# Second half's first two query/key/value column groups by seven products, and two weight buffers allocated ahead of a third

## The chip, the cores and the metric

The kernel runs on one core of one Trainium2 chip. The metric is the device time of one execution in microseconds, from three runs. The engines are TensorE (PE; its weight loads are listed as PEld), VectorE (DVE), ScalarE (ACT), GpSimd (POOL) and SyncE (SP), which here issues the DMAs.

## What is computed

A transformer block whose attention and MLP run side by side on the same layer norm; 2048 tokens, width 576, 32 heads of 18, 8 keys per query at a dilation of 2, hidden width 4608.

```python
xn = _layernorm(x)
q, k, v = (xn @ wqkv) split into 32 heads of 18
idx = pos[:, None] - 2 * arange(8)[None, :]
o = softmax(q . k[idx] * 18 ** -0.5) . v[idx]
attention = o.reshape(S, 576) @ wo
h = xn @ w1 + b1
mlp = (h * tanh(softplus(h))) @ w2
out = x + attention + mlp
```

## The kernel before

**Precision.** Every float32 matrix is held as a high and a low part. A product of two 128-deep tiles is three matmuls (high by high, low by high, high by low). The depth of 576 is four tiles of 128 and a remainder of 64, whose high and low rows share one tile, so that it costs two matmuls. A full product of 128 tokens with 432 columns is thus 4 x 3 + 2 = 14 matmuls.

**Stages.** The 2048 tokens are two halves (`hf` 0 and 1), a half is two blocks `b` of 512, a block is four token tiles `jj` of 128. In each half the program normalises and transposes the tokens (`norm1`, `ln_transpose`, tags `ta` and `tb`), makes q, k and v, and runs the MLP in 18 quads of 256 hidden columns: `m1_part` makes the hidden products (tags `h`), activates them, and `p_item` multiplies by w2 (tags `po`). The last `p_item` chunks of half 0 stand at the start of half 1's q/k/v work. The output projection of the attention comes last.

**q, k, v.** The 1728 columns are four groups `g` of 432. `qkv_item` makes one group of one token tile directly (14 matmuls, tags `pq`); ACT copies the result out of the accumulator. In both halves groups 0 and 1 go this way, and groups 2 and 3 go by Strassen's scheme with seven products in Winograd's form: the two blocks of 512 tokens, the two groups and the two halves of the depth make a 2 x 2 problem. One token tile of it takes seven products of six or eight matmuls, 50 in all, where four direct products take 56. It needs sums of the tokens (`S`, made by `s_step` on POOL, `s_high` on ACT, `s_low` on DVE) and sums of the weights (tags `y`, made at the start of half 0). Half 0 runs it with `za_part`, product by product over all token tiles: B11, B21, T2, T3, T4, T1, B22. Half 1 runs it with `z_part`, token tile by token tile, with weights that half 0 wrote to DRAM (`z_fetch`). A result that starts a q/k/v tile is copied by ACT, one that is added to it is added by DVE; `qkv_send` then stores it to DRAM.

**Attention.** A generator, stepped at listed places of the plan (`STEPS`, `SUMS`). For eight pairs of units per half POOL multiplies q by k (`pr`) and weights by v (`pv`), DVE reduces (`L`, `og`) and does the softmax's sums, ACT the exponentials. The last pairs of half 0 run beside half 1's q/k/v work.

**What sets the order.** The program is a list `plan` of PE's work in slots. `before(slot, fn)` hangs loads, casts, sums and steps on slots, and the tables `MOVED`, `STEPS`, `SUMS` and `AHEAD` shift single ones. Every engine executes what it was given in the written order. All DMAs go through one SP queue in order, and each waits also for one of eight semaphores in turn, so no more than eight are under way. Line numbers below are those of the kernel before.

**Buffers.** The weights of a quad's hidden products lie in `wa` (two buffers `wa0`, `wa1` of 5120 bytes per partition, written as separate tags), `t` (width 4 tiles) and `wc`. A tag's place is fixed when its first buffer is allocated. The tag `r3`, a 3456-byte weight buffer of the seven products, is allocated first; in the built program it starts at byte 206400 of each partition, `wa0` at 209856 and `wa1` at 217280. Counted from a multiple of 256, `wa0` and `wa1` start 192 bytes on; `r3`, `t`, `wc`, the token tiles `xt` and the sums `S` start 64 bytes on.

Of the kernel before, what the change touches and what calls it, by code (L numbers as in the profile page):

```python
# [18 lines left out]
P = 128  # L19
NH = 2  # L20
SH = S // NH
NB = 2
# [19 lines left out]
 108: (0, 0),  # L42
 117: (1, 1),
 122: (1, 1),
 131: (0, 1, 0),
 138: (0, 0),
 143: (0, 0),
 144: (0, 0),
 217: (0, 0),
 238: (-2, 1),  # L50
 282: (0, 0),
 389: (0, 0),
 424: (0, 0),
 430: (-1, 1),
 489: (0, 0),
 535: (0, 0),
 617: (1, 1),
 619: (1, 1),
 632: (0, 0),
 649: (1, 1),  # L60
 650: (-2, 1),
 692: (-1, 1),
 749: (0, 0),
 757: (0, 0),
 761: (0, 0),
 766: (-2, 0),
 789: (0, 0),
 810: (1, 1),
 815: (-1, 1),
 849: (0, 0),  # L70
 856: (0, 0),
 860: (-1, 1),
 887: (0, 0),
 889: (0, 0),
 945: (0, 0),
 957: (0, 0),
 961: (0, 0),
 997: (0, 0),
 1001: (2, 1),
 1011: (0, 1, 0),  # L80
 1012: (0, 0),
 1023: (0, 0),
 1025: (-2, 0),
 1041: (2, 1),
 1050: (1, 1),
 1071: (0, 0),
 1162: (0, 0),
 1184: (1, 1),
 1191: (0, 0),
 1208: (0, 0),  # L90
 1218: (2, 1),
 1221: (-2, 1),
 1229: (0, 1, 0),
 1253: (1, 1),
 1307: (0, 0),
 1328: (0, 0, 0)}


STEPS = ((36, 41, 47, 49, 53, 57, 63, 67, 70, 77, 78, 83, 85, 91, 95, 98, 105, 107, 111, 117, 123, 127, 130, 137, 139, 143,
# [7 lines left out]
SUMS = {(0, 0): (38, 0),  # L107
# [3 lines left out]
 (0, 33): (174, 0),  # L111
 (0, 59): (237, 0),
 (1, 5): (267, 0),
 (1, 8): (276, 0),
 (1, 10): (279, 0),
 (1, 28): (324, 0),
 (1, 35): (340, 0),
 (1, 38): (346, 0),
 (1, 46): (371, 1),
 (1, 50): (382, 1),  # L120
 (1, 54): (392, 0),
 (1, 56): (397, 1)}
AHEAD = (35, 37, 39, 40, 80, 84, 173, 184, 233, 234, 239, 240, 242, 244, 301, 318, 320, 339, 340, 416, 417)
# [7 lines left out]
def block_kernel(ctx: ExitStack, tc: tile.TileContext, x, wq, wo, w1, b1, w2, mask, out):  # L131
# [154 lines left out]
    def ln_transpose(hf, b, jj):  # L286
# [6 lines left out]
        if b == 0:  # L293
            nc.gpsimd.tensor_copy(rem, xn[:, KT * P:])
        else:
            nc.gpsimd.tensor_tensor(out=rem, in0=rem, in1=xn[:, KT * P:], op=ALU.subtract)
# [27 lines left out]

    def new(kind, hf, i):
        tag, bufs, width = home(kind, i)
        if tag == "wc":
# [110 lines left out]
    def qkv_item(hf, g, b, jj, mid=None, mid_at=4):  # L438
# [7 lines left out]
        if (g, b, jj) == (NQ - 1, 0, JB - 1):  # L446
            pq = ps.tile([P, 512], F32, tag="out", bufs=4, name=f"pq_{n}_{jj}")
        else:
            pq = ps.tile([P, 512], F32, tag="h", bufs=4, name=f"pq_{n}_{jj}")
# [13 lines left out]
        if jj == JB - 1:  # L463
            if (hf, g, b) == (1, 1, 1):
                zq["send"] = lambda: qkv_send(hf, g, b, kvs, qs)
            else:
                qkv_send(hf, g, b, kvs, qs)
# [66 lines left out]
    def za_part(n, half):  # L534
        X0, X1 = XTs[0, 0], XTs[0, 1]
        name = YORDER[n]
        src, hi, lo, rest = {"B11": (X0, 0, 5, None), "B21": (X0, 2, 7, (X0, 4, "R2")), "T2": (Ss.get((0, 1)), 0, 2, None),
                             "T3": (X1, 0, 5, None), "T4": (X1, 2, 7, (X1, 4, "R2")),
                             "T1": (Ss.get((0, 0)), 0, 2, (X1, 4, "R3")),
                             "B22": (Ss.get((0, 2)), 0, 2, (X1, 9, "R3"))}[name]  # L540
        to, add_ = {"B11": ((2, 0), 0), "B21": ((2, 0), 1), "T2": ((2, 1), 0), "T3": ((3, 1), 0), "T4": ((2, 1), 1),
                    "T1": ((3, 1), 1), "B22": ((3, 0), 0)}[name]
        if half == 0 and not add_:
            yq[to] = (sb.tile([P, 2 * UQ, JB, CU], F32, tag="w2", bufs=4, name="ykv_%d_%d" % to),
                      sb.tile([P, (TJ + HALO) * CU], F32, tag="kv", bufs=4, name="yqs_%d_%d" % to)[
                          :, 0:UQ * JB * CU].rearrange("p (u j c) -> p u j c", u=UQ, j=JB))
        kvs, qs = yq[to]
        for jj in (2 * half, 2 * half + 1):
            tok = slice(jj * P, (jj + 1) * P)
            if name == "B11":  # L550
                yq["h1", jj] = ps.tile([P, 512], F32, tag="out", bufs=4, name=f"y1_{jj}")[:, 0:432]
            elif name in ("B21", "T3"):
                yq["h3", jj] = ps.tile([P, 512], F32, tag="h", bufs=4, name=f"y{name}_{jj}")[:, 0:432]
            h = yq["h3" if name in ("B21", "T3", "T4") else "h1", jj]
            seq = [(src[:, xs + k, tok], yw[name, k][:, wl]) for k in range(2) for xs, wl in ((hi, 0), (lo, 0), (hi, 1))]
            if rest is not None:
                seq += [(rest[0][:, rest[1], tok], yw[rest[2], 0][:, wl]) for wl in range(2)]
# [9 lines left out]
        if half and (add_ or name == "B22"):  # L567
            qkv_send(0, *to, kvs, qs)
# [15 lines left out]

    def z_part(hf, jj, part):
        X0, X1 = XTs[hf, 0], XTs[hf, 1]
        tok = slice(jj * P, (jj + 1) * P)
        if part == 0:
            if jj == 0:
                for g in (2, 3):  # L590
                    for b in range(NB):
                        zq[g, b] = (sb.tile([P, 2 * UQ, JB, CU], F32, tag="w2", bufs=4, name=f"zkv_{g}_{b}"),
                                    sb.tile([P, UQ, JB, CU], F32, tag="xn", bufs=XNB, name=f"zqs_{g}_{b}"))
            if jj == JB - 1:
                zq["h"] = [ps.tile([P, 512], F32, tag="out", bufs=4, name=f"z{n}_{jj}")[:, 0:432] for n in (1, 3)]
                zq["h"].append(ps.tile([P, 512], F32, tag="h", bufs=4, name=f"z2_{jj}")[:, 0:432])
            else:
                zq["h"] = [ps.tile([P, 512], F32, tag="h", bufs=4, name=f"z{n}_{jj}")[:, 0:432] for n in (1, 3, 2)]
        h1, h3, h2 = zq["h"]
        S1, S2, S4 = (Ss[hf, n] for n in range(3))  # L600

        def mul(h, X, hi, lo, name, first, rest=None):
            seq = [(X[:, xs + k, tok], zw[name, k][wl]) for k in range(2) for xs, wl in ((hi, 0), (lo, 0), (hi, 1))]
            if rest is not None:
                seq += [(rest[0][:, rest[1], tok], zw[rest[2], 0][wl]) for wl in range(2)]
            for n, (l, r_) in enumerate(seq):
                nc.tensor.matmul(h, l, r_, start=first and n == 0, stop=n == len(seq) - 1, skip_group_check=True)  # L607

        def views(g, b, h):
            kvs, qs = zq[g, b]  # L610
            return ((kvs[:, :, jj, :], h[:, 0:288].rearrange("p (u c) -> p u c", u=2 * UQ)),
                    (qs[:, :, jj, :], h[:, 288:432].rearrange("p (u c) -> p u c", u=UQ)))

        def snap(g, b, h):
            for d, v in views(g, b, h):
                nc.scalar.copy(d, v)

        def plus(g, b, h):
            for d, v in views(g, b, h):
                nc.vector.tensor_tensor(out=d, in0=v, in1=d, op=ALU.add)  # L620

        def send(g, b):
            if jj == JB - 1:
                qkv_send(hf, g, b, *zq[g, b])
        if part == 0:
            mul(h1, X0, 0, 5, "B11", True)
            snap(2, 0, h1)
            mul(h2, X0, 2, 7, "B21", True, (X0, 4, "R2"))
            plus(2, 0, h2)
            send(2, 0)  # L630
        elif part == 1:
            mul(h1, S2, 0, 2, "T2", False)
            snap(2, 1, h1)
            mul(h3, X1, 0, 5, "T3", True)
            snap(3, 1, h3)
        elif part == 2:
            mul(h1, S1, 0, 2, "T1", False, (X1, 4, "R3"))
# [1151 lines left out]
```

## Time and profile before

| what | value |
|---|---|
| three runs | 1113.59, 1114.18, 1112.23 us (median 1113.59) |
| the profiled execution's own time | 1110.76 us |
| its span, first to last instruction | 1109.0 us |
| granted TensorE clock | 0.998 |
| busy: PE, PEld | 1094.4 us (99%), 1005.4 us (91%) |
| busy: DVE, POOL, ACT | 874.6 us (79%), 780.1 us (70%), 508.7 us (46%) |
| DMA | 276.01 MB, mean 249 GB/s |

Profile and prediction use times from the span's start. In a group's row, `out<-in` are the tiles written and read; "idle" is the time for which the engine stood still just before, with what it then waited for. A window's row gives each engine's busy time in that stretch and the number of its instructions, then the granted clock, the DMA engines' busy share and their rate.

### The profile page before, as it was taken

Reading aid. Unit: us, or ns where it says so; the run is one execution under the profiler, and the core shown is the slowest. Engines: PE = TensorE matmul, PEld = TensorE weight load, DVE = VectorE, ACT = ScalarE, POOL = GpSimd, SP = SyncE. Lnnn points to the kernel's source line nnn. Section 1 sums busy time; section 2 is a strip of 40 time slices with the busy share of each in tenths; the row PEclk is TensorE's granted clock in tenths of the full one; section 3 lists DMA queues with packets and bytes.
Section 4 is the critical chain, followed back from the end, with each engine's and each line's share of the span. In section 5 each row is a group of like instructions: output and inputs, shape, how many; then the busy total and the mean of one; then the engine's idle time right before and its main releaser. Section 6 shows DMA issues by size and latency. Waiting matters only on the chain.

```text
span 1109.0 us, 18148 instructions
## 1 busy us (share of the span) xinstructions
PE 1094.4 (99%) x6478; PEld 1005.4 (91%) x6478; DVE 874.6 (79%) x1433; ACT 508.7 (46%) x935; POOL 780.1 (70%) x635
## 2 busy tenths in 40 slices
PE   8999999999999999999999999999999999989998
PEld 8998899999999999999998889989999989989998
DVE  6775888898987888987756568887888895787786
ACT  5554554454456444454333354444444434243353
POOL 2434967878776776867679669778676799967442
PEclk9999999999999999999999999999999999999999
DMA  6769997867877586666598899675668476487864
GB/s 225 271 232 344 358 327 247 273 241 265 273 250 249 209 280 220 232 251 203 186 303 276 272 339 337 239 237 200 212 216 266 167 241 219 152 292 243 252 218 141
DMA packets 183006, 276.01 MB, mean 249 GB/s; under 512 B 53346, under 2 KB 124292, under 8 KB 182916
## 3 DMA queue, kind: packets, MB, share of 16 engines
q1 hardware_dynamic: 182916, 274.86, 73.4%
q8 instruction: 51, 0.84, 0.3%
q14 instruction: 39, 0.32, 0.1%
HBM read 162.16 MB, written 112.66 MB: 248 GB/s over the span
## 4 chain that ended last, share of the span: by engine, by line
PE 92%; DMA 2%; DVE 2%; issue 1%; POOL 1%; SPq 1%; ACT 0%; DVEq 0%; ACTq 0%; POOLq 0%
PE h L834 29%; PE po L936 21%; PE po L1028 12%; PE pq L459 7%; PE po L1049 6%; PE h L840 6%; PE o L1232 5%; PE z L607 4%; PE y L559 1%; PE yT L559 1%; PE yB L559 1%; DMA pw<-kept_T 1%; DMA kept_yB<-yw_B 1%; DMA w<-kept_w 1%; PE ta L166 0%
## 5 line engine op out<-in xcount | busy, mean ns | idle before, releaser
L936 PEld LDWEIGHTS po<-w,act 128*128 128x128 f32 x1728 | 236.5, 188 | 5.7
L936 PE MATMUL po<-w,act 128*128 128x288 f32 x1728 | 240.6, 295 | 0.0
L697 POOL TENSOR_TENSOR pr<-q,kv 128x576 f32<-128x576 f32 x128 | 195.6, 1553 | 10.2 <-DMA q<-q_d 4.6
L736 POOL TENSOR_TENSOR pv<-L,kv 128x576 f32<-128x576 f32 x128 | 176.5, 1477 | 31.6 <-DVE L L729 14.5
L886 POOL TENSOR_TENSOR act<-c,act 128x512 fp32r<-128x512 f32 x69 | 93.7, 1358 | 99.6 <-ACT act L885 94.1
L1028 PEld LDWEIGHTS po<-pw,u 128*128 128x128 f32 x1008 | 138.3, 188 | 5.5 <-issue 1.9
L1028 PE MATMUL po<-pw,u 128*128 128x288 f32 x1008 | 140.7, 295 | 1.5 <-DMA pw<-kept_T 1.5
L940 DVE TENSOR_TENSOR acc<-po,acc 128x288 f32<-128x288 f32 x288 | 118.5, 449 | 23.1 <-PE po L936 21.8
L834 PE MATMUL h<-xt,t 128*128 128x512 f32 x432 | 111.3, 392 | 2.1 <-ACT t L365 1.5
L834 PE MATMUL h<-S,t 128*128 128x512 f32 x432 | 110.4, 391 | 0.1
L834 PE MATMUL h<-xt,wa 128*128 128x512 f32 x432 | 106.2, 395 | 0.0
L880 ACT ACTIVATE c<-c,b1c 128x512 f32<-128x512 f32 x69 | 50.0, 725 | 121.5 <-DVE c L879 121.3
L742 DVE TENSOR_REDUCE og<-pv 128x144 f32<-128x1152 f32 x64 | 86.0, 1345 | 19.4 <-POOL pv L736 19.3
L702 DVE TENSOR_REDUCE L<-pr 128x64 f32<-128x1152 f32 x64 | 85.9, 1342 | 17.6 <-POOL pr L697 17.5
L834 PEld LDWEIGHTS h<-xt,wa 128*128 128x128 f32 x432 | 81.3, 189 | 18.5
L834 PEld LDWEIGHTS h<-xt,t 128*128 128x128 f32 x432 | 79.0, 188 | 18.1 <-ACT t L365 1.9
L459 PE MATMUL pq<-wq,xt 128*128 128x432 f32 x448 | 91.8, 362 | 0.8 <-ACT xt L172 0.7
L834 PEld LDWEIGHTS h<-S,t 128*128 128x128 f32 x432 | 78.0, 188 | 13.4 <-ACT rm L868 0.5
L459 PEld LDWEIGHTS pq<-wq,xt 128*128 128x128 f32 x448 | 83.0, 188 | 5.6 <-ACT xt L172 1.1
L1049 PEld LDWEIGHTS po<-w,act 128*128 128x128 f32 x576 | 79.9, 191 | 5.0 <-DVE accP L1052 3.4
L1049 PE MATMUL po<-w,act 128*128 128x288 f32 x576 | 81.2, 298 | 2.9 <-DVE accP L1052 2.9
L868 ACT COPY c<-h 128x512 f32<-128x512 f32 x69 | 40.4, 585 | 86.5 <-PE h L840 43.5
(259 smaller groups left out, 1989.2 us busy)
## 6 DMA issues: line engine op xcount, KB each, us to landing
kv<-kv_d SPq DMA_DIRECT2D x64, 396.0 KB, 6.1
kept_t<-t SPq DMA_DIRECT2D x36, 512.0 KB, 4.1
t<-kept_t SPq DMA_DIRECT2D x36, 512.0 KB, 4.6
pw<-kept_T SPq DMA_DIRECT2D x24, 576.0 KB, 6.1
rw<-in_w SPq DMA_DIRECT2D x36, 320.0 KB, 5.0
kept_wa<-wa SPq DMA_DIRECT2D x18, 640.0 KB, 4.6
wa<-kept_wa SPq DMA_DIRECT2D x18, 640.0 KB, 5.2
rw<-in_w SPq DMA_DIRECT2D x36, 288.0 KB, 5.7
```

The source lines that it names most:

```text
L459: nc.tensor.matmul(pq[:, 0:432], XT[:, xi, tok], wt[wi][:, hl, 0:432], start=i == 0, stop=i == len(seq) - 1)
L697: nc.gpsimd.tensor_tensor(out=pr[:, x:x + hh], in0=q[:, j0 + x:j0 + x + hh, None, :].to_broadcast([P, hh, W, CU]), in1=win(kt, 0, CU, j0 + ...
L702: nc.vector.tensor_reduce(L[:, k, j0:j0 + hj].rearrange("p j w h -> p (j w h)"), pr.rearrange("p j w (h d) -> p (j w h) d", h=2), axis=AX, ...
L736: nc.gpsimd.tensor_tensor(out=pr[:, x:x + hj].rearrange("p j d w -> p j w d"), in0=L[:, k, x:x + hj, :, h:h + 1].to_broadcast([P, hj, W, DH]),
L742: nc.vector.tensor_reduce(og[:, c0:c0 + DH, :].rearrange("p d j -> p j d"), pr, axis=AX, op=ALU.add)
L834: nc.tensor.matmul(ph, wt[:, wl, wk * P:(wk + 1) * P], X[:, xs, :], start=first and i == 0, stop=last and i == len(seq) - 1, skip_group_ch ...
L840: nc.tensor.matmul(ph, wt[:, wl, off * P:(off + 1) * P], X[:, xs, :], start=False, stop=wl == 1, skip_group_check=True)
L886: nc.gpsimd.tensor_tensor(out=a[:, 1, :], in0=t, in1=a[:, 0, :].bitcast(F32), op=ALU.subtract)
L936: nc.tensor.matmul(po, acts[hf, q, b, j][:, al, tok], done["w2", hf, 2 * q + j][:, wl, c * HC:(c + 1) * HC], start=i == 0, stop=i == 5)
L940: nc.vector.tensor_tensor(out=t, in0=po, in1=t, op=ALU.add)
L1028: nc.tensor.matmul(po, units[e, k, qq][:, al, tok], w[:, qq, wl, :], start=i == 0, stop=i == 5)
L1049: nc.tensor.matmul(po, acts[hf, q, b, j][:, al, tok], done["w2", hf, 2 * q + j][:, wl, c * HC:(c + 1) * HC], start=i == 0, stop=i == 5)
```

## The change

1. **Groups 0 and 1 of half 1 by seven products.** New weight sums are made during half 0's last quads: `z_load` loads raw weights (8 loads of 216 KB), `z_sum` takes 8 differences of 128x432 on POOL, `z_high` casts them on ACT, `z_low` takes the low parts on DVE, `z_keep` stores both to DRAM (16 stores of 216 KB). `v_fetch` loads the 16 weight buffers of 432 KB in half 1, in place of ten loads of that size.
2. **`za_part` serves all three.** `which` is "y" (half 0), "v" (half 1, groups 0 and 1) or "z" (half 1, groups 2 and 3). `z_part` goes. In half 1 the seven products now run product by product as well. The last product of "z", B22, is done for two token tiles before the quads; the other two are put into quads 0 and 1 (before: one token tile, in quad 1).
3. **Block 1's transposes in half 1** now stand between the last four `p_item` chunks, ahead of all q/k/v work. Their remainder copy moves from POOL to ACT, and the subtraction from POOL to DVE; each `x_load` moves one step ahead.
4. **The token sums of half 1** follow one another on POOL, ahead of the `pv` products of attention pair 5.
5. **`reserve`**: `wa0`, `wa1`, `og` and `oT` are allocated before `r3`. In the built program `wa0` now starts at byte 206400 and `wa1` at 211520, both 64 bytes past a multiple of 256; `r3` at 221248.
6. **The tables** are new throughout; outside the stretch above they shift single instructions of DVE, ACT, POOL and SP, while PE's order stays as it was.

The core of the diff, without the tables:

```diff
     def norm1(n):
-        nc.gpsimd.tensor_copy(xn[:, D:D + 64], xn[:, KT * P:D])
+        (nc.scalar.copy if n >= JB else nc.gpsimd.tensor_copy)(xn[:, D:D + 64], xn[:, KT * P:D])
+        if n >= JB:
+            rem = rems[1][:, n - JB, :]
+            nc.vector.tensor_tensor(out=rem, in0=rem, in1=xn[:, KT * P:], op=ALU.subtract)
...
+    def reserve():
+        for i in range(2):
+            early[f"wa{(i + 1) % 2}"] = sb.tile([P, 2, 5 * P], F32R, tag=f"wa{(i + 1) % 2}", bufs=1, name=f"wa_0_{i}")
+        early["og"] = sb.tile([P, PU * CU, TJ], F32, tag="og", bufs=1, name="og_0")
+        early["oT"] = sb.tile([P, PU * CU * TJ], F32, tag="oT", bufs=1, name="oT_0_0")
...
     def za_high(name, k=0):
         tag = YHOME[name][k]
+        if tag == "r3":
+            reserve()
...
-    def za_part(n, half):
+    def za_part(which, n, half, jjs=None):
+        hf, g0, w = {"y": (0, 2, yw), "v": (1, 0, vw), "z": (1, 2, zw)}[which]
...
+    def z_sum(name, k):
+        nc.gpsimd.tensor_tensor(out=vraw[name, k], in0=vraw[x, k], in1=vraw[y, k], op=ALU.subtract)
+    def z_high(name, k):
+        nc.scalar.copy(hi, vraw[name, k])
+    def z_low(name, k):
+        nc.vector.tensor_tensor(out=t.bitcast(F32R), in0=t, in1=hi.bitcast(F32), op=ALU.subtract)
+    def v_fetch(name, k):
+        t = vw[name, k] = sb.tile([P, 2, 432], F32R, tag=tag, bufs=BUFS[tag], name=f"vw_{name}_{k}")
+        nc.sync.dma_start(t.rearrange("p h c -> p (h c)").bitcast(F32),
+                          vkept[name, k] if name[0] == "T" else kept["wq", v_unit(name, k)])
...
-    def z_part(hf, jj, part):
...
             tr(0, 3)
-            pr_(0, NP - 1, *CHUNKS[0])
-            pr_(0, NP - 1, *CHUNKS[1])
-            for jj in range(JB):
-                qi(1, 0, 0, jj)
-                if jj < 2:
-                    pr_(0, NP - 1, *CHUNKS[2 + jj])
-                if jj:
-                    tr(1, jj - 1)
-            for g, b in ((0, 1), (1, 0), (1, 1)):
-                for jj in range(JB):
-                    qi(1, g, b, jj)
-                    if (g, b, jj) == (0, 1, 0):
-                        tr(1, 3)
-        if hf:
-            for jj in range(JB):
-                for part in range(4):
-                    if jj < JB - 1 or part not in (3,):
-                        zi(jj, part)
+            for k in range(4):
+                pr_(0, NP - 1, *CHUNKS[k])
+                tr(1, k)
+            for which in "vz":
+                for n in range(len(YORDER)):
+                    for half in range(2):
+                        if (which, n, half) != ("z", len(YORDER) - 1, 1):
+                            yi(n, half, which)
```

Three places of the new order follow. First PE at the start of half 1. Before, from the last half of the `p_item` chunks (`po`) on, a direct q/k/v item (`pq`) stands between chunks, and the transposes of block 1 (`ta`, `tb`) between the items:

```order
L936 MATMUL po_17_0_3_1_6441<-w_0_34_5910,act_0_34_5945 128x288 x3
L936 MATMUL po_17_0_3_1_6441<-w_0_35_6012,act_0_35_6223 128x288 x3
L166 MATMUL ta_6454<-ident,xn_4_47_6083 128x128 x4
L167 MATMUL tb_6455<-ident,xn_4_47_6083 128x128
L169 MATMUL tb_6455<-ident,rem_6058 128x128
L459 MATMUL pq_0_0_2_6471<-wq_0_6014,xt_0_6057 128x432 x3
L459 MATMUL pq_0_0_2_6471<-wq_1_6144,xt_0_6057 128x432 x3
L459 MATMUL pq_0_0_2_6471<-wq_2_6209,xt_0_6057 128x432 x3
L459 MATMUL pq_0_0_2_6471<-wq_3_6016,xt_0_6057 128x432 x3
L459 MATMUL pq_0_0_2_6471<-wq_4_6238,xt_0_6057 128x432 x2
```

Now, behind the same last chunk, the last transpose of block 1, then the first of the seven products (`v`, weights `vw`), six matmuls per token tile:

```order
L1004 MATMUL po_17_0_3_1_6517<-w_0_34_5984,act_0_34_6016 128x288 x3
L1004 MATMUL po_17_0_3_1_6517<-w_0_35_6077,act_0_35_6298 128x288 x3
L237 MATMUL ta_6528<-ident,xn_7_52_6275 128x128 x4
L238 MATMUL tb_6529<-ident,xn_7_52_6275 128x128
L240 MATMUL tb_6529<-ident,rem_6117 128x128
L649 MATMUL v_0_6552<-vw_B_0_6347,xt_0_6116 128x432 x3
L649 MATMUL v_0_6552<-vw_B_1_6349,xt_0_6116 128x432 x3
L649 MATMUL v_1_6561<-vw_B_0_6347,xt_0_6116 128x432 x3
L649 MATMUL v_1_6561<-vw_B_1_6349,xt_0_6116 128x432 x3
```

All four transposes of block 1 have moved ahead of the first q/k/v product; before, the last of them stood behind five direct items.

Second, POOL. Before, behind the `pv` products of pair 5, the token sums (`s`) lie between the products of pair 6:

```order
L736 TENSOR_TENSOR pv_5_1_1_6505<-L_5_5993,kv_0_11_6130 128x4x8x18 x2
L296 TENSOR_TENSOR rem_6058<-rem_6058,xn_6_51_6220 128x128
L296 TENSOR_TENSOR rem_6058<-rem_6058,xn_7_53_6274 128x128
L697 TENSOR_TENSOR pr_6_0_0_6590<-q_12_6354,kv_0_12_6352 128x576 x2
L789 TENSOR_TENSOR s_60_6615<-s_54_6453,xt_0_6057 128x512
L789 TENSOR_TENSOR s_60_6615<-s_60_6615,xt_0_6057 128x512
L697 TENSOR_TENSOR pr_6_0_1_6649<-q_12_6354,kv_0_12_6352 128x576 x2
L789 TENSOR_TENSOR s_61_6680<-xt_0_6057,s_60_6615 128x512
```

Now the fourteen sums stand together, ahead of pair 5's `pv` (the last four sums and what follows them):

```order
L857 TENSOR_TENSOR s_65_6601<-s_65_6601,xt_0_6116 128x512
L857 TENSOR_TENSOR s_66_6631<-xt_0_6116,xt_1_6351 128x512
L857 TENSOR_TENSOR s_u_6632<-xt_0_6116,xt_1_6351 128x512
L857 TENSOR_TENSOR s_66_6631<-s_66_6631,s_u_6632 128x512
L803 TENSOR_TENSOR pv_5_0_0_6716<-L_5_6144,kv_0_10_6149 128x4x8x18 x2
L803 TENSOR_TENSOR pv_5_0_1_6761<-L_5_6144,kv_0_10_6149 128x4x8x18 x2
L803 TENSOR_TENSOR pv_5_1_0_6804<-L_5_6144,kv_0_11_6198 128x4x8x18 x2
L803 TENSOR_TENSOR pv_5_1_1_6830<-L_5_6144,kv_0_11_6198 128x4x8x18 x2
```

The attention of pair 5 thus waits on POOL for the whole block of sums.

Third, SP in the new program, where the weights of product T1 (the two `vw_T` rows) are fetched; `zacc` are weights of the "z" products, `kv` and `q` the attention's inputs:

```order
L697 DMA vw_T_0_6706<-kept_vT_0_5018 128x864
L708 DMA zacc_B_1_6708<-kept_yB_1_847 128x432
L708 DMA zacc_B_1_6709<-kept_yB_1_847 128x432
L719 DMA kv_0_12_6719<-kv_d_129 128x792
L728 DMA q_12_6721<-q_d_133 128x288
L719 DMA kv_0_13_6764<-kv_d_129 128x792
L728 DMA q_13_6766<-q_d_133 128x288
L697 DMA vw_T_1_6768<-kept_vT_1_5567 128x864
```

T1's second half stands behind six other loads; before, no seven-product weights of these groups were fetched here.

More of the change, by code (lines that the diff above doesn't have):

```diff
@@ new lines @@
+ 834: (0, 0),
+ 855: (1, 1),
+ 860: (-1, 1),
+ 894: (0, 0),
+ 901: (0, 0),
+ 905: (-1, 1),
+ 932: (0, 0),
+ 934: (0, 0),
+ 990: (0, 0),
+ 1002: (0, 0),
+ 1006: (0, 0),
+ 1042: (0, 0),
+ 1046: (2, 1),
+ 1056: (0, 1, 0),
+ 1057: (0, 0),
+ 1068: (0, 0),
+ 1070: (-2, 0),
+ 1086: (2, 1),
+ 1095: (1, 1),
+ 1101: (2, 1),
+ 1104: (2, 1),
+ 1106: (0, 0),
+ 1107: (2, 1),
+ 1116: (0, 0),
+ 1121: (0, 0),
+ 1122: (1, 0),
+ 1160: (-2, 1),
+ 1161: (-3, 1),
+ 1164: (1, 1),
+ 1166: (-2, 1),
+ 1201: (0, 1, 0),
+ 1207: (0, 0),
@@ L108 @@
+SUMS = {(0, 0): (42, 1),
+ (0, 1): (38, 0),
  (0, 11): (86, 0),
@@ L583, in z_fetch @@
             zw[name, k] = [t[:, 0], t[:, 1]]
-    def z_part(hf, jj, part):
[L586 to L637, printed above, removed]
-            plus(3, 1, h1)
-            send(3, 1)
-            mul(h3, X1, 2, 7, "T4", False, (X1, 4, "R2"))
-            plus(2, 1, h3)
-            send(2, 1)
-        else:
-            mul(h1, S4, 0, 2, "B22", False, (X1, 9, "R3"))
-            snap(3, 0, h1)
-            send(3, 0)
```

302 lines of the change are left out of this document (184 added, 118 removed), and 18 rows, old and new, of tables (STEPS, i).

## The prediction

> **What bounds the kernel now.** I read the busy shares first, then the chain that ended last (the page):
>
> ```profile
> PE 1094.4 (99%) x6478; PEld 1005.4 (91%) x6478; DVE 874.6 (79%) x1433; ACT 508.7 (46%) x935; POOL 780.1 (70%) x635
> PE 92%; DMA 2%; DVE 2%; issue 1%; POOL 1%; SPq 1%; ACT 0%; DVEq 0%; ACTq 0%; POOLq 0%
> ```
>
> PE is busy for all but 15 us and makes 92% of the chain. So a matmul removed is time gained, unless a wait takes its place; work added to DVE, ACT or POOL costs only where it makes PE wait. PE's waits, longest first (line, releaser, total us, times, longest):
>
> ```profile
> PE po L1049 <- DVE accP L1052: 2.9, 1, 2.9
> PE po L1028 <- DMA pw<-kept_T: 1.5, 1, 1.5
> PE h L834 <- ACT t L365: 1.5, 1, 1.5
> ...
> PE z L607 <- ACT zqs L616: 0.9, 1, 0.9
> ...
> PE z L607 <- DVE zqs L620: 0.8, 1, 0.8
> ```
>
> They are short and single. The first two lie near 971 and 897 us, in the second half's w2 work, whose PE order isn't changed; I leave them as they are. Which engine would be next in the changed stretch is read from the windows (busy us of PE, PEld, DVE, ACT, POOL, then clock, DMA share, GB/s):
>
> ```profile
> 430.00:480.00 50.00, 50.00 (x300) 45.56 (x299) 43.38 (x60) 21.71 (x35) 42.70 (x36) 1.00 0.64 221
> 480.00:526.46 46.46, 46.46 (x296) 42.98 (x295) 39.12 (x65) 23.89 (x41) 33.05 (x35) 1.00 0.71 240
> 526.46:555.68 29.22, 29.22 (x191) 28.37 (x191) 21.34 (x38) 11.53 (x27) 20.30 (x25) 1.00 0.58 188
> 555.68:586.00 30.32, 30.32 (x157) 29.01 (x156) 19.00 (x21) 9.88 (x30) 23.79 (x18) 1.00 1.00 314
> 586.00:626.00 40.00, 38.32 (x194) 36.00 (x193) 25.41 (x42) 10.62 (x35) 33.03 (x25) 1.00 0.76 255
> 626.00:680.00 54.00, 53.95 (x275) 45.92 (x274) 36.08 (x46) 26.19 (x46) 40.95 (x31) 1.00 1.00 340
> ```
>
> DVE and POOL have room everywhere, the DMA engines have none from 556 to 586 and from 626 to 680. The clock is whole throughout.
>
> **The matmuls.** The chain in order of time (start, us, what) gives the price of one:
>
> ```profile
> 526.46 6.36 PE po L936 x48
> ...
> 544.72 0.44 PE ta L166 x4
> 545.16 0.11 PE tb L167
> 545.27 0.11 PE tb L169
> ...
> 555.68 30.26 PE pq L459 x154
> ...
> 591.33 0.39 ACT zkv L616
> ...
> 595.41 0.46 DVE zkv L620
> ...
> 596.14 29.73 PE z L607 x150
> ```
>
> 30.26 / 154 is 196 ns for a matmul of 432 columns in the direct form, 29.73 / 150 is 198 in the seven products: the same. Sixteen direct items of 14 are 224, four token tiles of 50 are 200, and 24 x 196 ns is **-4.7 us**. The "z" products keep their 200; deferring a second token tile of B22 into quad 0 moves eight matmuls and removes none.
>
> **The waits in the "z" products.** The last rows show PE held from about 591.1 to 592.0 by ACT's copy out of an accumulator and from 595.4 to 596.1 by DVE's addition: 0.9 and 0.8. The old order handles one token tile at a time with three accumulators, so a product reuses what the last but one has just left. In the new order four token tiles stand between two uses of an accumulator, at least 18 matmuls or 3.6 us. I take both waits as gone, **-1.7** (0 to -1.7); what may be late next is counted as new waits.
>
> **An early wait that the tables touch.** At the first quads of half 0 PE stands twice (timeline of PE):
>
> ```profile
> 114.19 0.74 PE L834 MATMUL h<-xt,t 128*128 128x512 f32 x2 [1.47 <-ACT t L365]
> 115.58 1.20 PE L834 MATMUL h<-xt,t 128*128 128x512 f32 x4 [0.65 <-DVE t L366]
> ```
>
> ACT's own rows say why:
>
> ```profile
> 112.24 0.72 ACT L880 ACTIVATE c<-c,b1c 128x512 f32<-128x512 f32 x1 [1.61 <-DVE c L879]
> ...
> 113.52 0.61 ACT L365 CAST t<-tt 128x512 fp32r<-128x512 f32 x1
> ```
>
> The last row is the cast of `t` that PE needs; it is queued behind an activation that waits for DVE. In the new order this cast stands ahead of that activation, so it could run up to 2.1 us sooner; DVE's low part still has to follow. I take half, **-1.0** (0 to -2.1).
>
> **The place of `wa`.** The hidden matmuls by the weights that they take (min/median/max ns), at L834, then at L840:
>
> ```profile
> L834 PE MATMUL h<-xt,wa x432: 389/393/405, 94.7 to 1017.2; 128*128 128x512 f32 x144
> ...
> L834 PE MATMUL h<-xt,t x432: 387/389/504, 99.3 to 1029.9; 128*128 128x512 f32 x144
> ```
>
> ```profile
> L840 PE MATMUL h<-xt,wa x144: 389/396/405, 97.5 to 1030.4; 128*128 128x512 f32 x144
> L840 PE MATMUL h<-xt,wc x144: 389/389/398, 102.1 to 1035.5; 128*128 128x512 f32 x144
> ```
>
> The same operation on the same tokens is 4 ns longer with `wa` than with `t`, and 7 ns longer with `wa` than with `wc`. What sets `wa` apart in the program is its place, 192 bytes past a multiple of 256 where the others are 64 past, and that is what `reserve` changes. If it is the cause, 432 x 4 + 144 x 7 ns = 2.7 us go. No row shows `wa` anywhere else, so the ends are 0 and -2.7, and below nothing is excluded by `r3`, which keeps its 64 bytes. Both pairs of rows agree, so I take the whole, **-2.7**.
>
> These loads into the array are listed by the page:
>
> ```profile
> L834 PEld LDWEIGHTS h<-xt,wa 128*128 128x128 f32 x432 | 81.3, 189 | 18.5
> L834 PEld LDWEIGHTS h<-xt,t 128*128 128x128 f32 x432 | 79.0, 188 | 18.1 <-ACT t L365 1.9
> ```
>
> 189 ns against 188: the load itself hardly tells the tiles apart. The Trainium skill, "TensorE: Matmul & The Clock Gate", section "LDWEIGHTS (loading the stationary operand)", lets a weight load depend on the number of its columns alone; by that rule the place of `wa` gives nothing and the sum is 2.7 smaller. The loads' rows agree with it, the matmuls' rows do not, and I follow the latter, since they are what PE's time is made of.
>
> **What is added beside PE.** During half 0's last quads POOL gets eight differences of 432 columns; the nearest row is the second here, a token sum of 512 columns on POOL between 526 and 626 (the first, an attention product, is used further down):
>
> ```profile
> L697 POOL TENSOR_TENSOR pr<-q,kv 128x576 f32<-128x576 f32 x19 | 27.7, 1481 | 1.7 <-DVE og L742 1.7
> L789 POOL TENSOR_TENSOR s<-s,xt 128x512 f32<-128x512 f32 x6 | 8.1, 1351 | 0.3
> ```
>
> 1351 x 432 / 512 is 1.14 us, eight are 9; POOL has 7 us free in 430 to 480 and 13 in the next window, with PE at 100%. DVE's eight low parts are like those of the token sums (min/median/max ns):
>
> ```profile
> L820 DVE TENSOR_TENSOR S<-s,S x12: 677/688/1914, 47.2 to 591.5; 128x512 fp32r<-128x512 f32 x12
> ```
>
> That is 5 us for eight at the median, up to 15 at the longest; ACT's eight casts, 0.61 for the cast of 512 columns above, are 5. I cost all this at nothing; if the cover were gone at one place, one POOL difference, 1.1 us, would show. In half 1 the sixteen q/k/v copies on ACT stay sixteen, and twelve additions of 0.75 us on DVE are new, 9 us; DVE idles 34 us in the three windows from 526 to 626.
>
> **New waits.** Chunks and transposes now fill 4 x 3.18 + 4 x 0.66 = 15.4 us from 526.5, so "v" starts at 541.8; at 4.75 us for a product of six matmuls per tile and 6.3 for one of eight, T1 starts at 568.7 and "z" at 581. Three things can be late. The last transpose needs ACT's norm, which is queued behind a cast of a token sum, and DVE's subtraction: 0 to 0.8. The third token sum (T3 and after it B22) has little margin behind fourteen sums in a row, 14 x 1.35 = 19 us of POOL: 0 to 2. T1's second weights take the buffer of T3's first, free about 561.8, and are needed at 569.3. Such loads take (KB each, median us to landing, from 586 on):
>
> ```profile
> z_T<-kept_yT SPq DMA_DIRECT2D x2, 432.0 KB, 6.2
> ```
>
> 561.8 + 6.2 is 568.0, 1.3 us in time, if the six loads ahead of it on SP have been issued: 0 to 4. Together 0 to 6; I take **+2.0**, 0.8 for the transpose and 1.2 for the load.
>
> **The sum.** -4.7 - 1.7 - 1.0 - 2.7 + 2.0 = -8.1 us, from 1110.76 to 1102.7 for an execution like the profiled one. That one is 2.8 us under the median of the runs, so the median is forecast at **1105.5**.
>
> **The rivals.** *The place gives nothing.* Then -5.4, 1108.2. For it speaks that the loads' rows are alike; against it that both lines show the same excess. Chance 0.20.
>
> *Weights late.* Six loads more, 2.6 MB, or 7.6 us at 340 GB/s; the shares of 0.58 and 0.76 leave 12 and 10 us free, which speaks against it. But the windows between are full, and SP is in order: if T1's second weights land in 12 us rather than 6.2, T1 waits 4.5; with as much again for what is behind it in the queue (T1's remainder, B22), less what the later products recover, I put the new waits at 8 instead of 2, and the time is 1111.5. Chance 0.12.
>
> *DVE late behind POOL, slower than before.* Now DVE is in order and sits idle behind a `pr` (timeline; the groups from 526 to 626 follow):
>
> ```profile
> 576.86 1.35 DVE L702 TENSOR_REDUCE L<-pr 128x64 f32<-128x1152 f32 x1 [5.55 <-POOL pr L697]
> ```
>
> ```profile
> L702 DVE TENSOR_REDUCE L<-pr 128x64 f32<-128x1152 f32 x10 | 13.4, 1345 | 7.5 <-POOL pr L697 7.5
> ...
> L620 DVE TENSOR_TENSOR zkv<-z,zkv 128x288 f32<-128x288 f32 x12 | 5.5, 454 | 9.5 <-PE z L607 8.5 <-DMA z_B<-kept_yB 1.0
> ...
> L620 DVE TENSOR_TENSOR zqs<-z,zqs 128x144 f32<-128x144 f32 x11 | 3.3, 297 | 0.0
> ```
>
> An addition queued behind it holds PE's accumulator. The place is T4 and T1, eight token tiles in a row whose results are added, and B22 behind them in T1's accumulators. Where POOL's step (2 x 1.48), the reduce (1.35) and two additions (2 x 0.75) follow one another, a slot takes 5.8 us against PE's 16 x 0.198 = 3.2; four slots are 10.5 late, one product covers 4.75, and 5.8 remain, 11.5 for "v" and "z" together: -8.1 + 11.5 is +3.4, 1117.0. It decides the sign from 8.1 us of such waits, and can be told from no change from 10.3. Against it: POOL works ahead of DVE in most steps, and 7.5 us of idle behind `pr` in 100 us is little. Chance 0.10. The token sums' low parts read two tiles on DVE and took from 677 to 1914 ns for one shape, which would lengthen this chain further. The Trainium skill, "GPSIMD Engine Reference", section "Key points", has POOL contend with VectorE instructions of two such inputs; the spread fits that, though the row doesn't say what ran beside the long ones.
>
> **How the numbers follow.** The forecast has 0.58. Its best case is -4.7 - 1.7 - 2.1 - 2.7 = -11.2, a median of 1102.4, with another 1.4 by which the lowest run lay under the median: 1101. The upper end takes in the second case and most of the third: 1112.5; the fourth is left out with what lies beyond these ends. A measurement can tell about 0.2%, 2.2 us. Faster by more: the first two cases and a third of the third, 0.82; within: the rest of it, 0.08; slower: 0.10.
>
> **What would show it.** PE's count falls by 24; the 432-column matmuls of half 1 stay at 196 to 198 ns; the quads begin at 617.6 plus the new waits instead of 625.9 (4.7 from the matmuls, 1.6 from the deferred tile, 1.7 from the waits); `wa` rows read 389 like `t`; the wait at 114 is at most half. Wrong it would be by a wait of PE for `vw` or `z` weights, or for DVE's additions, of more than 2 us in all between 541 and 621, or by quads after 626 that wait for a DMA, since everything then comes earlier to a queue that is full.

## The result, and the profile after

| | before | changed |
|---|---|---|
| median of the runs | 1112.91 us (4 runs, 1112.15 to 1114.18) | 1101.12 us (4 runs, 1099.32 to 1102.50) |
| ratio | | 0.9896, 95% interval 0.9884 to 0.9908 |
| profiled execution, span | 1110.76, 1109.0 us | 1099.32, 1097.5 us |
| granted clock in it | 0.998 | 1.000 |

The changed kernel is 11.8 us faster where 8.1 was forecast (1105.5). A second comparison gave 0.9904 (0.9882 to 0.9925). Two executions that lie far off all others, 2783.34 us of the kernel before and 1175.89 us of experiment 11's kernel, are left out of every ratio. Single runs of either kernel differ by 5 us, so differences of 2 us or less are read from the profiles below, not from the times.

The page's busy shares and the list of PE's waits, after:

```profile
PE 1085.5 (99%) x6454; PEld 999.2 (91%) x6454; DVE 883.8 (81%) x1469; ACT 512.8 (47%) x947; POOL 789.6 (72%) x635
```

```profile
PE po L1117 <- DVE accP L1120: 3.3, 1, 3.3
...
PE v L649 <- DMA vw_T<-kept_vT: 1.1, 1, 1.1
...
PE po L1004 <- DVE acc L1008: 0.6, 1, 0.6
```

PE's busy time fell by 8.9 us (24 matmuls fewer) and its idle time from 14.6 to 12.0. The two "z" waits and the two waits near 114 us are not in the list any more; new are 1.1 us for T1's weights (`v`) and 0.6 at a `p_item` chunk (`acc`). The chain through the changed stretch, after:

```profile
538.24 4.94 PE v L649 x24
543.18 6.27 PE vB L649 x32
549.45 4.75 PE v L649 x24
554.19 6.29 PE vT L649 x32
560.49 6.35 DMA vw_T<-kept_vT
...
566.88 12.22 PE v L649 x61
579.11 4.72 PE z L649 x24
583.82 6.28 PE zB L649 x32
590.10 4.71 PE z L649 x24
594.81 11.01 PE zT L649 x56
605.81 9.42 PE z L649 x48
615.23 2.73 PE h L902 x12
```

Each product takes the forecast 4.7 or 6.3 us, all of "z" runs without a wait, and the only break is the load of T1's second weights: issued at 560.49, landed 6.35 later, 1.1 us after PE needed it. The quads begin at 615.2 instead of 625.9.

The hidden matmuls by their weights, after, at L902 and then at L908:

```profile
L902 PE MATMUL h<-xt,wa x432: 387/389/497, 94.7 to 1005.8; 128*128 128x512 f32 x144
...
L902 PE MATMUL h<-xt,t x432: 387/389/501, 99.3 to 1018.5; 128*128 128x512 f32 x144
```

```profile
L908 PE MATMUL h<-xt,wa x144: 388/389/398, 97.5 to 1018.9; 128*128 128x512 f32 x144
L908 PE MATMUL h<-xt,wc x144: 388/389/397, 102.0 to 1023.9; 128*128 128x512 f32 x144
```

`wa` now reads like the others. Last, PE around 114 us and around 964 us:

```profile
112.41 1.86 PE L902 MATMUL h<-xt,t 128*128 128x512 f32 x6
```

```profile
964.06 3.44 PE L1117 MATMUL po<-w,act 128*128 128x288 f32 x24 [3.27 <-DVE accP L1120]
```

The same place in the profile of before, in PE's timeline:

```profile
973.62 4.97 PE L1049 MATMUL po<-w,act 128*128 128x288 f32 x24 [2.95 <-DVE accP L1052]
```

Behind a wait of 3 us the 24 matmuls took 4.97 us before and 3.44 in the profile after. The granted clock of that stretch was 0.65 before and 1.00 after. This 1.5 us is part of the difference of the two profiles. The wait stands in twelve of the profiles taken here, 2.55 to 3.28 us long: in the four with a mean clock of 1.000 the 24 matmuls behind it took 3.44 or 3.45 us, in the eight with 0.997 or 0.998 they took 4.97 to 6.13. So the mean clock of a run is a sign of whether it met this drop.

### The profile page after: what moved, and what is told of

It is laid out like the page before. It is cut to its first block, busy times and chain, and to the rows that moved or that the text cites. A ratio compares the mean times of both kernels' runs of the same rounds, so it can differ in the third digit from the quotient of the medians.

```text
span 1097.5 us, 18210 instructions
## 1 busy us (share of the span) xinstructions
PE 1085.5 (99%) x6454; PEld 999.2 (91%) x6454; DVE 883.8 (81%) x1469; ACT 512.8 (47%) x947; POOL 789.6 (72%) x635
## 4 chain that ended last, share of the span: by engine, by line
PE 92%; DMA 3%; DVE 2%; issue 1%; ACT 1%; POOL 0%; POOLq 0%; SPq 0%
PE h L902 29%; PE po L1004 21%; PE po L1096 11%; PE po L1117 7%; PE h L908 5%; PE o L1300 5%; PE pq L540 3%; PE y L649 2%; PE z L649 2%; PE v L649 2%; PE zT L649 1%; PE yT L649 1%; DMA pw<-kept_B 1%; DMA pw<-kept_T 1%; DMA vw_T<-kept_vT 1%
## 5 line engine op out<-in xcount | busy, mean ns | idle before, releaser
L803 POOL TENSOR_TENSOR pv<-L,kv 128x576 f32<-128x576 f32 x128 | 172.0, 1450 | 42.3 <-DVE L L796 19.8
L902 PE MATMUL h<-xt,t 128*128 128x512 f32 x432 | 111.0, 391 | 0.1
L902 PE MATMUL h<-S,t 128*128 128x512 f32 x432 | 110.6, 391 | 0.1
L902 PE MATMUL h<-xt,wa 128*128 128x512 f32 x432 | 104.0, 389 | 0.0
L902 PEld LDWEIGHTS h<-xt,wa 128*128 128x128 f32 x432 | 80.9, 188 | 16.8 <-DMA wa<-kept_wa 0.3
L902 PEld LDWEIGHTS h<-xt,t 128*128 128x128 f32 x432 | 79.0, 188 | 15.4 <-DVE t L450 0.5
L902 PEld LDWEIGHTS h<-S,t 128*128 128x128 f32 x432 | 77.9, 188 | 13.8 <-ACT rm L936 0.4
L1102 DVE TENSOR_TENSOR accP<-po,accP 128x288 f32<-128x288 f32 x156 | 63.2, 448 | 15.9 <-PE po L1096 7.9
L947 DVE TENSOR_TENSOR c<-h,c 128x512 f32<-128x512 f32 x69 | 47.1, 683 | 23.9 <-PE h L908 20.7
```

Source lines behind the costliest of these rows:

```text
L803: nc.gpsimd.tensor_tensor(out=pr[:, x:x + hj].rearrange("p j d w -> p j w d"), in0=L[:, k, x:x + hj, :, h:h + 1].to_broadcast([P, hj, W, DH]),
L902: nc.tensor.matmul(ph, wt[:, wl, wk * P:(wk + 1) * P], X[:, xs, :], start=first and i == 0, stop=last and i == len(seq) - 1, skip_group_ch ...
L1102: nc.vector.tensor_tensor(out=t, in0=po, in1=t, op=ALU.add)
```

## The experiments

**1. The early allocation taken back** (`no_reserve`), from the changed kernel:

```diff
-        if tag == "r3":
-            reserve()
```

> The changed kernel without the early allocation: the first weight block's buffers wa0 and wa1 lie 192 bytes past a multiple of 256 again. Theory (the place costs 4 ns per matmul at one line and 7 at the other): the wa rows read 393 and 396 ns instead of 389, PE is busy 2.7 us longer, time about 1103.8 against 1101.1. Rival (the wa rows of the kernel before were long for another reason, its order or its loads): the rows stay at 389 and the time at 1101.1.

Measured: 1104.07 us, ratio 0.9912 (0.9887 to 0.9937). The `wa` rows of its profile:

```profile
L900 PE MATMUL h<-xt,wa 128*128 128x512 f32 x432 | 106.3, 395 | 0.5 <-DMA wa<-kept_wa 0.5
...
L906 PE MATMUL h<-xt,wa 128*128 128x512 f32 x144 | 45.5, 397 | 0.0
```

After the change they are 104.0 and 44.4 us. So the place costs 2.3 + 1.1 = 3.4 us of PE time. By the medians the kernel is 3.0 us slower, by the two ratios 1.8; the intervals overlap, so the rows show the cost and the times do not.

**2. The early allocation alone** (`before_reserve`): `reserve` and its call put into the kernel before, nothing else.

> The kernel before with the early allocation alone. Theory (the place): wa rows fall to 389 ns, PE busy 2.7 us less, time about 1110.2 against 1112.9 (ratio 0.9976). Rival (the place does nothing by itself): rows stay at 393 and 396, ratio 1.000. That the allocation gives more than its matmuls show: ratio under 0.996.

Measured: 1106.80 us, ratio 0.9940 (0.9922 to 0.9958). The rows of its profile:

```profile
L847 PE MATMUL h<-xt,wa 128*128 128x512 f32 x432 | 103.8, 389 | 0.0
...
L853 PE MATMUL h<-xt,wa 128*128 128x512 f32 x144 | 44.4, 389 | 0.0
```

Against 106.2 and 45.5 before, that is 3.5 us. The time fell by 6.8 us, with an interval from 4.7 to 8.7, and the profiled execution by 4.8 (1110.76 to 1105.92). The warming matmuls at the start are 0.6 us shorter in this profile, but PE then waits 0.7 us longer for the first transpose, and the first hidden product starts at 94.8 us against 94.7 before; they are no part of it. The third case of the expectation, more than the matmuls show, holds: 1.2 us or more beyond them is not explained. DVE's busy time also fell, 874.6 to 869.0 us, and `og` and `oT` moved as well; whether that is the rest wasn't tried.

**3. One buffer at each place** (`split`): only `wa1` is reserved, `wa0` is allocated later. These are the tags of the code: the buffer at byte 206400 in the changed kernel, which "The change" calls `wa0`, has the tag `wa1`.

```diff
-        for i in range(2):
+        for i in range(1):
             early[f"wa{(i + 1) % 2}"] = ...
```

> The changed kernel with only wa1 allocated early; wa0 comes after the 3456-byte buffer. In the program wa1 (even quads' or odd quads' blocks, alternating) starts 64 bytes past a multiple of 256 and the other 192 past, in one run. Theory (the place of each buffer): the wa rows fall into two kinds that alternate by quad, 12 matmuls in 2.72 to 2.74 us for one and 2.78 to 2.80 for the other, PE busy about 1.35 us more than in the changed kernel. Rival (something common to both buffers): all quads alike.

Measured in a single run: 1102.62 us. The buffer reserved starts at byte 206400, 64 past a multiple of 256; the other at 223936, 192 past. Three successive quads in PE's timeline (start, us to the modelled end, twelve matmuls; the step to the next row is the exact time):

```profile
158.06 2.95 PE L902 MATMUL h<-xt,wa 128*128 128x512 f32 x12
160.85 0.62 PE L908 MATMUL h<-xt,wa 128*128 128x512 f32 x2
...
182.26 2.88 PE L902 MATMUL h<-xt,wa 128*128 128x512 f32 x12
184.98 0.61 PE L908 MATMUL h<-xt,wa 128*128 128x512 f32 x2
...
206.35 2.95 PE L902 MATMUL h<-xt,wa 128*128 128x512 f32 x12
209.14 0.62 PE L908 MATMUL h<-xt,wa 128*128 128x512 f32 x2
```

2.79, 2.72, 2.79 us: the long and the short alternate with the buffer, in one run, and do so through the rest of the trace but for one quad at the start of half 1 (2.77). In the changed kernel all quads but two take 2.72 or 2.73, in the kernel before all take 2.78 or 2.79. The place is the cause.

**4. A third place** (`pad_96`): 32 unused bytes between the two reserved buffers.

> The changed kernel with 32 unused bytes between the first weight block's two buffers: wa0 stays 64 bytes past a multiple of 256, wa1 lies 96 past. Theory (only some places cost: 192 does, 64 does not): no forecast for 96; if what counts is the byte within 128, 64 and 192 would be the same place, which the split kernel excludes. If 96 is like 64, all quads read 2.72 us for 12 matmuls; if it is like 192 or worse, every second quad reads 2.79 or more, PE busy 1.7 us or more over the changed kernel.

Measured in a single run, 1103.89 us. Two successive quads (read as above):

```profile
182.34 2.88 PE L904 MATMUL h<-xt,wa 128*128 128x512 f32 x12
185.06 0.61 PE L910 MATMUL h<-xt,wa 128*128 128x512 f32 x2
...
206.43 2.96 PE L904 MATMUL h<-xt,wa 128*128 128x512 f32 x12
209.22 0.63 PE L910 MATMUL h<-xt,wa 128*128 128x512 f32 x2
```

The quads alternate between 2.72 us (the buffer 64 bytes past) and 2.79 (the one 96 past), as in the split kernel. By the code's tags these are `wa1` and `wa0`; the expectation has the two names the other way round. A start 96 past costs what 192 does. Other starts weren't tried.

**5. 24 matmuls put back** (`b11_twice`):

```diff
+            for _ in range(2 if (which, name) == ("v", "B11") else 1):
                 for i, (l, r_) in enumerate(seq):
                     nc.tensor.matmul(h, l, r_, ...)
```

> The changed kernel with the first product of groups 0 and 1 (B11) computed twice, the second time over the first: 24 matmuls of 432 columns put back, all else kept. Theory (PE alone bounds this stretch, so a matmul costs its 196 ns): the quads of half 1 begin 4.7 us later, time about 1105.8. Rival (part of the stretch is set by weights or by DVE, so that added PE work is hidden there): the wait for the second weights of T1 (1.1 us) stays gone or smaller and 3.6 us or less are lost, 1104.7 or below.

Measured: 1104.54 us, ratio 0.9918 (0.9899 to 0.9936), 3.4 us over the changed kernel; in the profiles, both at clock 1.000, 1102.8 against 1097.5 us of span, 5.3. The quads began at 620.67 instead of 615.23. Its waits of PE in this stretch:

```profile
PE z L650 <- DVE qs_z L655: 1.3, 1, 1.3
PE ta L237 <- ACT xn L356: 1.0, 2, 0.8
```

The wait for T1's weights went, as the rival had it, which gives 1.1 us back; a "z" wait for DVE of 1.3 us and 0.7 us more at the transposes came in its place. With the 4.7 us of the matmuls that accounts for the 5.4 us by which the quads are later, to 0.2. In this profile the matmuls cost their price and were not hidden; the times, 3.4 us apart by the medians and 2.4 by the ratios, are those that the rival named.

**6. The attention's first steps at their old places** (`steps_back`):

```diff
-STEPS = ((33, 36, 47, ...
+STEPS = ((36, 41, 47, ...
```

> The changed kernel with the first two attention steps of half 0 at their old places (36 and 41 instead of 33 and 36), so that the kv and q loads of the first pair and POOL's first product come as late as before; ACT's order around the t cast of quad 1 stays the new one (t cast ahead of the activation). Theory (ACT's order freed PE at 112 to 115 us): the wait stays gone, no difference in the first 130 us beyond 0.5 us. Rival (the earlier attention step freed it, because the reduce on DVE no longer waits for POOL): PE waits about 2.1 us again near 114 and everything behind lies 2 to 2.5 us later.

Measured: 1103.84 us, ratio 0.9938 (0.9917 to 0.9959). The row at 112 us in PE's timeline:

```profile
112.87 1.86 PE L902 MATMUL h<-xt,t 128*128 128x512 f32 x6
```

No wait there, and the next rows lie 0.46 us later than in the changed kernel (114.57 against 114.11). So the earlier attention step did not free PE, and ACT's order, with the `t` cast ahead of the waiting activation, is what is left of the two causes; no run puts the cast alone back. The time is longer by 2.7 us by the medians and 4.7 by the ratios. The profile shows that this arises later: 1.5 us behind the 3 us wait (4.98 against 3.44, clock 0.998) and waits of single us (1.4 for `c`, 0.8 more at `acc`); I did not follow them.

**7. Another buffer for T1's second weights** (`t1_wb`):

```diff
-        tag = YHOME[name][k]
+        tag = "wb" if (name, k) == ("T1", 1) else YHOME[name][k]
         t = vw[name, k] = ...
```

> The changed kernel with the second weights of T1 (groups 0 and 1) in the tag wb, whose buffers are free after B21, instead of the buffer of T3's first weights. Theory (the wait of 1.1 us at 565.8 is for that buffer, then for the landing): the load is issued some 8 us earlier, the wait goes, the quads begin 1.1 us earlier, time about 1100.0. Rival (the queue was full, so the load lands late all the same, or the wait moves to the next product): the quads begin at the same time.

Measured: 1101.57 us, ratio 0.9901 (0.9880 to 0.9921). PE still waited, for the same load (timeline of PE, then of SP):

```profile
568.12 0.85 PE L649 MATMUL v<-vw_T,S 128*128 128x432 f32 x3 [1.70 <-DMA vw_T<-kept_vT]
```

```profile
560.60 0.96 SPq L728 DMA_DIRECT2D q<-q_d  x1
561.60 0.70 SPq L697 DMA_DIRECT2D vw_T<-kept_vT  x1
```

The theory of the buffer falls; the load is late all the same, as the rival had it. It is issued directly behind the `q` load ahead of it on SP, as in the changed kernel, though its new buffer has been free since B21. That leaves its place in SP's order, or a queue that is full, which is the rival's reason; experiment 12 decides between them.

**8. One low part later** (`low_later`). PE's longest wait, 3.3 us at 960 (2.9 at 971 before), is in both kernels. DVE's rows there, changed kernel:

```profile
952.48 1.35 DVE L769 TENSOR_REDUCE L<-pr 128x64 f32<-128x1152 f32 x1 [2.10 <-POOL pr L764]
953.75 8.03 DVE L1201 TENSOR_TENSOR raw_T<-raw_T,woh_T 128x576 fp32r<-128x576 f32 x2
```

Two low parts of the output projection's weight sums took 8.03 us and held the additions PE waited for. The second was moved two slots later:

```diff
+ 1333: (2, 1),
+ 1334: (1, 1),
```

> The changed kernel with the low part of the output projection's second sum (raw_T) on DVE two slots later, behind the additions to accP that follow. Theory (PE's wait of 3.3 us at 960 is for two such low parts in a row of 4 us each, beside POOL): one goes behind the additions, the wait falls to 0 to 0.5 us, time 1097.5 to 1098; where the wait also lowers the granted clock, another 1.6 us in those runs. Rival (DVE is late there by its reduces anyway): 2 us or more of the wait stay.

Measured: 1100.26 us, ratio 0.9894 (0.9876 to 0.9911). The wait fell to 2.6 us only. DVE and POOL in its timeline:

```profile
952.74 7.36 DVE L1203 TENSOR_TENSOR raw_T<-raw_T,woh_T 128x576 fp32r<-128x576 f32 x1
...
965.50 0.75 DVE L1203 TENSOR_TENSOR raw_T<-raw_T,woh_T 128x576 fp32r<-128x576 f32 x1
```

```profile
952.54 2.93 POOL L766 TENSOR_TENSOR pr<-q,kv 128x576 f32<-128x576 f32 x2
955.32 1.39 POOL L956 TENSOR_TENSOR act<-mn,act 128x512 fp32r<-128x512 f32 x1
956.58 2.90 POOL L766 TENSOR_TENSOR pr<-q,kv 128x576 f32<-128x576 f32 x2
962.18 1.28 POOL L956 TENSOR_TENSOR act<-c,act 128x512 fp32r<-128x512 f32 x1 [2.70 <-ACT act L955]
```

The wait that stays is as long as the rival said, but the cause is neither the theory's (4 us each) nor the rival's (the reduces): one operation took all of it. It started 0.2 us after POOL's first product and ended 0.6 us after POOL's last, and the same operation takes 0.75 us while POOL idles.

**9. Both edits** (`t1_wb_low_later`).

> Both of these edits together. If the two waits are independent, 4.4 us less than the changed kernel in the profile, time about 1096.7 (ratio to the kernel before about 0.985); if one of them is taken up by another wait, 1098 to 1100.

Measured: 1099.99 us, ratio 0.9897 (0.9879 to 0.9915), with waits of 2.6 us for `accP` and 1.3 for `vw_T` left. As each edit alone left its wait, this tells nothing more.

**10. The changed kernel again** (`after_again`).

> The changed kernel itself once more, beside the next two on one chip. All theories: ratio to the kernel before 0.9884 to 0.9908 as in the first comparison, about 1101 us. If this comparison differs by more than 0.2% from the first, the differences between kernels of separate comparisons can't be read to 2 us.

Measured: 1102.54 us, ratio 0.9904 (0.9882 to 0.9925), six runs from 1099.07 to 1104.56. Its three runs at clock 1.000 took 1099.1 to 1101.7, the three at 0.997 or 0.998 took 1103.4 to 1104.6. Both comparisons agree within 0.1%.

**11. Both low parts later** (`lows_later`):

```diff
+ 1330: (4, 1),
+ 1331: (3, 1),
+ 1333: (2, 1),
+ 1334: (1, 1),
```

> The changed kernel with both low parts (raw_T) behind the additions to accP and the next reduce, where POOL has no products to run. Theory (one such low part, 0.75 us alone, can't proceed while POOL's two-input products follow one another without a gap; moving one away left 7.36 us for the other): both take 0.75 us each, PE's wait of 3.3 us goes to 0 to 0.3, and so does the drop of the clock behind it (1.6 to 2.8 us): spans 1093 to 1094.5, time about 1096. Rival (DVE is late by something else there): 2 us or more of the wait stay, 1099 to 1100.

Measured: 1099.36 us (the median of the four runs compared), ratio 0.9888 (0.9868 to 0.9908), profiled span 1094.5. DVE and PE at the place:

```profile
962.21 1.42 DVE L1205 TENSOR_TENSOR raw_T<-raw_T,woh_T 128x576 fp32r<-128x576 f32 x2
```

```profile
960.12 3.33 PE L1121 MATMUL po<-w,act 128*128 128x288 f32 x24
964.20 1.65 PE L906 MATMUL h<-S,t 128*128 128x512 f32 x6 [0.75 <-ACT c L940]
```

1.42 us for both, and the wait of 3.3 us is gone; ACT makes PE wait 0.75 instead. The clock was 1.000 in all of the four runs compared. The spans of the two profiles differ by 3.0 us (1097.5 to 1094.5), of which these waits are 2.5. The times, 1096.2 to 1101.6 in those four runs, lie in the middle above the 1096 of the theory; they alone do not separate this kernel from the changed one.

**12. And T1's second weights earlier on SP** (`lows_t1`), on top of 11 and 7:

```diff
-("R3", 0, 4), ("T1", 0, 6), ("T1", 1, 8),
+("R3", 0, 4), ("T1", 1, 4), ("T1", 0, 6),
```

> The same with T1's second weights issued on SP ahead of the kv and q loads (into a buffer of the tag wb, free by then). Theory (in the new order this load was issued at 560.5 behind six others, and only that made it late): it is issued near 555, lands near 562, PE's wait for vw_T of 1.1 to 1.7 us goes: time about 1.1 us under the kernel with the low parts alone. Rival (the DMA engines are full there, so what goes ahead makes another load late): no gain, the wait turns up at the next weights (T1's first, B22) or in the z products.

Measured: 1097.51 us, ratio 0.9862 (0.9842 to 0.9881), the fastest of all; the changed kernel beside it had 0.9904. The load's row on SP:

```profile
555.00 2.53 SPq L701 DMA_DIRECT2D vw_T<-kept_vT  x1
```

PE no longer waits for `vw_T`, but once, 1.4 us, for a DVE addition in "z":

```profile
PE z L653 <- DVE qs_z L658: 1.4, 1, 1.4
```

Issued at 555.0 instead of 560.5 the load is in time, beside the same other loads, so its place in the order was the cause of the wait, not a full queue; in this profile the gain went to the next wait, as in experiment 5. In span this profile, 1097.3, is no better than that of 11, so the second edit's own gain is not shown. That both together beat the changed kernel is, by 0.4%, with intervals that lie side by side without overlapping (up to 0.9881 and from 0.9882).

## Why the prediction was right or wrong

The direction, the bound and the likeliest case held; 1101.1 lies at the low end of the range, 0.1 us inside it, because two terms were mis-sized and one was missing. Term by term, the difference of the two profiled spans (-11.5):

| term | forecast | profiles | from |
|---|---|---|---|
| matmuls | -4.7 | -4.7 | 24 fewer, each still 196 ns; put back, experiment 5 |
| waits in "z" | -1.7 | -1.7 | no longer listed |
| wait near 114 | -1.0 | -2.1 | both rows, 1.47 and 0.65, gone |
| place of `wa` | -2.7 | -3.3 | busy 106.2 to 104.0 and 45.5 to 44.4 |
| new waits | +2.0 | +1.7 | 1.1 for `vw_T`, 0.6 at `acc` |
| clock behind the 3 us wait | none | -1.5 | 4.97 to 3.44 |
| all else | none | +0.1 | remainder |

- **The matmuls**, the largest term, came out as worked out.
- **The place of `wa`**: the mechanism was right, and experiments 3 and 4 show it. The size was off because I took the difference of the medians (4 and 7 ns); the means in the lists differ by 6 and 8 (395 and 397 against 389), and PE's time is made of means. The rival that it gives nothing is refuted: the matmuls got shorter, though the loads of the same weights hardly changed (189 to 188 ns on average, and 188 with the old place in experiment 1). Why a matmul takes longer while its load doesn't is not shown. By the times, the allocation is worth 4.7 to 8.7 us in the kernel before; what it does beyond its matmuls stays open.
- **The wait near 114**: I took half on the ground that DVE's low part would still be late. It was not. Experiment 6 rules out the earlier attention step as the cause; the cast's place in ACT's order is what remains.
- **The new waits** had the right sum, and the load of T1 was the right one. But the reason given for it, the buffer of T3's first weights, was wrong: with another buffer (7) it stayed late, and only its place in SP's order moved it (12).
- **The clock** was not in the sum. The wait that I set aside as unchanged (2.9 us, 3.3 after) cost more than itself: 1.5 us of slower matmuls in the profile of before. That the profile after has none is in part luck: three of the six runs of experiment 10 were at 0.997 or 0.998. Of 33 runs of the kernel before, made beside the experiments, one was at 1.000; of ten runs of the changed kernel five. Why it is spared more often wasn't tried. In experiment 10 the three runs below 1.000 have a median 7.8 us under that of the kernel before beside them (1104.52 against 1112.31, all ten of those runs below 1.000), which is about the forecast, and the three at 1.000 lie 12.9 under; in the first comparison the two below 1.000 lie 11.0 under. How much of the miss is the clock is thus not settled by the times.
- **The start of the quads**, forecast at 617.6 plus the new waits, was 615.2. The three terms named beside it make 617.9, not 617.6, and they left out what half 0 gains, the wait near 114 (2.1) and half of `wa`'s term (1.7). 617.9 + 1.7 - 3.8 is 615.8; the other 0.6 was not traced.
- **Weights late**: one load was, by 1.1 us, not 6. **DVE late behind POOL**, the slower rival: not at T4 and T1, where I put it; PE waited for no DVE addition in "v" or "z". The two engines do collide, but in the second half's w2 work, in both kernels (at 963 us before, at 953 after).

## What to carry to other kernels

In this kernel, whose matmul engine is busy 99% of the span, matmuls taken out were worth their full price, with four token tiles between two uses of an accumulator; the rest of the gain hides in rows that differ from rows of the same shape, so compare groups of one shape by their means and look at each group's longest instruction. When a load is late, read what was issued just ahead of it before blaming its buffer. A wait that both kernels share still belongs into the account, since what it does to the clock can differ from run to run.

## What the runs showed of the hardware

- **Where weights start matters to the matmul.** Twelve matmuls of 512 columns with weights 64 bytes past a multiple of 256 took 2.72 us, with weights 96 or 192 bytes past it 2.79 us, buffer by buffer within a run (experiments 3 and 4).
- **A DVE operation can be shut out by POOL altogether.** A subtraction of 576 columns with two inputs in SBUF took 0.75 us beside an idle POOL and 7.36 beside five POOL instructions in a row, ending 0.6 us after the last. It stands in the profile of before too, as the longest of its group (min/median/max ns):

```profile
L1133 DVE TENSOR_TENSOR raw_T<-raw_T,woh_T x4: 744/940/7344, 963.3 to 985.3; 128x576 fp32r<-128x576 f32 x4
```

The Trainium skill, "GPSIMD Engine Reference", section "Key points", names contention with such instructions; here it was exclusion until POOL paused. It isn't always so. Some 20 us later in the changed kernel the same operation came in between two POOL products without a pause (DVE, then POOL):

```profile
974.72 1.76 DVE L1201 TENSOR_TENSOR raw_T<-raw_T,woh_T 128x576 fp32r<-128x576 f32 x1
```

```profile
974.67 3.07 POOL L803 TENSOR_TENSOR pv<-L,kv 128x576 f32<-128x576 f32 x2
```

Two such products alone take 2.6 us. What decides whether DVE gets in behind one POOL instruction or only behind the last is not shown.
- **A wait of about 3 us can cost the clock.** Behind one of 3.27 us, 24 matmuls took 3.44 us in one profile of the changed kernel and 6.04 in another (3.34 elsewhere); behind 2.60 us they took 6.13 (experiment 8), behind 2.55 us 3.45 (experiment 9), and 3.34 with only a wait of 0.75 us ahead of them. With the wait gone, all eight runs compared of experiments 11 and 12 were at 1.000. The Trainium skill, "TensorE: Matmul & The Clock Gate", section "What's actually happening", has the clock set by activity windows of about 3.4 us that run freely, and throttled after at least one idle window. That one wait sometimes costs and sometimes doesn't fits windows that run freely; but waits of 2.60 to 3.27 us, shorter than a window, were followed by a drop here, so a whole idle window was not needed, and the rows decide.
